# Attention and gated network in one kernel: a planner that looks ahead, one more group computed apart, a changed order of two loops, and projections that wait for fewer transfers

## The chip, the core and the metric

One core of a Trainium2 chip runs the whole program. The metric is the device time of one execution, the median of several. The engines are TensorE (PE: products of matrices, with its weight loads shown as PEld), VectorE (DVE), ScalarE (ACT), GpSimd (POOL) and SyncE (SP), which here issues the transfers.

## What is computed

First a linear attention: 8 batches, 8 heads, 576 tokens, head size 64, 128 features. Its result, 4608 tokens by 512, goes through a gated network with 1536 hidden columns. The arrays that come from `q`, `k`, `v` and `w_phi` are float32, the weights of the network float64.

```python
def phi(x):
    proj = np.einsum('bhsd,df->bhsf', x, w_phi)
    proj = proj - np.max(np.abs(proj), axis=-1, keepdims=True)
    return np.concatenate([np.exp(proj), np.exp(-proj)], axis=-1)
q_p, k_p = phi(q), phi(k)
kv, z = np.einsum('bhsf,bhsd->bhfd', k_p, v), np.sum(k_p, axis=2)
num = np.einsum('bhsf,bhfd->bhsd', q_p, kv)
den = np.einsum('bhsf,bhf->bhs', q_p, z)[..., None] + 1e-06
x = (num / den)             # then laid out as (4608, 512)
g = x @ w_gate
out = (g * (1.0 / (1.0 + np.exp(-g))) * (x @ w_val)) @ w_out
```

## The kernel before

**Heads.** Two heads make a pair, and 32 pairs are worked off in order by `attention(i, rank)`. For a pair, SP loads the keys, values and queries (L455 to L464, L582); of keys and queries the main part, 512 columns, comes in a first transfer and the last 64 in two small ones, one for each head. TensorE projects keys and queries (L354) in groups of columns, the last group being the tail. VectorE takes the largest magnitude (L502, L613) and subtracts it (L507, L618), ScalarE makes the exponentials, and TensorE the sums over keys (L546) and the numerators and denominators (L710). Then follows a chain: ScalarE copies the denominators out (L732), VectorE transposes them (L743) and takes the reciprocal (L744), GpSimd spreads it to all partitions (L748, L753), VectorE transposes it back (L757) and multiplies (L759). The result is x. Since the products take reduced operands, x is kept as a high part `xh` (ScalarE) and a low part `xl` (VectorE, L784), or, for later tokens, stored whole to `x_dram` (L774).

**Chunks.** The network works on 12 chunks c of 384 tokens and 12 groups f of 128 hidden columns. The first three chunks are made of the first 8 pairs, the "early" ones, and these run ahead of everything. For chunks 0 to 3 `first(c, f, low)` makes gate and value (a = 0 and 1, in the two banks `ps_gv`, gv in the trace) from four quarters k of the model's columns, where quarter k comes from the pair k of a batch. Each (a, k) is three products of 384 columns: high by high, high by low, low by high. Then ScalarE takes the tanh, and VectorE's L863 and L866 read the two banks, which frees them. `second` makes the output (L887 is the low part of the hidden values).

**Weights.** `weight_piece` turns a group's float64 weights into a high and a low part: ScalarE's L380, and on VectorE L381, L383, L386, L389, L391, L394 and, after ScalarE's copy, L397. Pieces of gate and value weights have 1024 columns (tile `a`), pieces of output weights 512 (`spare` or `m`). They are made once, while the early pairs run and after, and stored to `w_dram` for later loads.

**Pairs of chunks.** Chunks 4 to 11 go two by two through `block(c, f, ...)`, which makes the products of two chunks out of seven instead of eight and joins them with sums (L1112 is its product, L1122 and L1125 copy and join, L1045 loads its weights, L1061 loads x from `x_dram`). The generator `shared` calls the blocks: chunks 4 and 5, then 6 and 7, each over all f; then the last two pairs of chunks together. For f under LEAD only c_a (8 and 9) is computed; for f from LEAD to 11 c_a and c_b (10 and 11) follow one another and share the loaded weights (`held`); then c_b is computed for the f under LEAD, with those weights loaded again. A second phase behind it makes their outputs (L1359 and further).

**What sets the order.** No engine's order is written out by hand. The kernel adds steps to a `Plan`, each with an engine, a cost, the steps it comes after, and a rank. `Plan.run` goes through time by these costs: whenever an engine is free, it takes the ready step of lowest rank, whatever will become ready a moment later. What comes out is the fixed order of instructions on each engine. The waits between engines in the program follow from the data that the instructions read and write. An early pair's steps have its number as rank, 0 to 7; the steps of the network have -1 (FIRST), its loads -0.5 (NEXT), the products on TensorE 1000 and above, weight pieces 5, 6.5 and from 7.1 on. URGENT is -0.8. When TensorE has nothing ready in the plan, a filler product (L1484, L1487) is put there.

The rule in `first` for the order of the (a, k):

```python
order = [(a, k) for ks in ((0, 1, 2), (3,)) for a in range(2) for k in ks] if f == 0 else \
    [(a, k) for a in range(2) for k in range(NK)]
```

so for f = 0 the quarter k = 3 of both halves comes after the other three of both.

Of the kernel before, what the change touches and what calls it, by code (L numbers as in the profile page):

```python
# [23 lines left out]
NF = 128  # L24
# [28 lines left out]
LEAD = 4  # L53
# [3 lines left out]
URGENT = -0.8  # L57
OFFSETS = (0, -1, 0, 0, 0)


class Step:
    __slots__ = ("eng", "cost", "fn", "left", "then", "rank", "n", "lag", "take", "give", "key", "early")

    def __init__(self, eng, cost, fn, rank, n, lag, take, give, key):
        self.eng, self.cost, self.fn, self.rank, self.n, self.lag = eng, cost, fn, rank, n, lag
        self.take, self.give, self.key = take, give, key
        self.left, self.then, self.early = 0, [], 0


class Plan:  # L70
# [33 lines left out]
    def run(self):  # L104
        ready = {e: [] for e in self.LAG}
        busy = dict.fromkeys(self.LAG, False)
        for s in self.steps:
            if not s.left:
                heapq.heappush(ready[s.eng], (s.key, s))
        events, n, wire = [], 0, 0.0  # L110
        now = 0.0

# [3 lines left out]
        def start(e):  # L116
            nonlocal n, wire
            held = []
            got, saved = None, False
            while ready[e]:  # L120
                key, s = heapq.heappop(ready[e])
                if s.take is not None and (saved or len(s.take) > sum(len(x) for x in self.lists(s))):
                    held.append((key, s))
                    saved = True
                    continue
                got = s
                break
            for h in held:
                heapq.heappush(ready[e], h)
# [21 lines left out]
            for t in s.then:  # L151
                n += 1
                heapq.heappush(events, (freed if t.eng == e and e in ("ACT", "DVE", "PE", "POOL") else done, n, "dep", t))
# [11 lines left out]
        while events:  # L165
            now = events[0][0]
            while events and events[0][0] <= now:
# [3 lines left out]
                elif kind == "dep":  # L171
                    x.left -= 1
                    if not x.left:
                        heapq.heappush(ready[x.eng], (x.key, x))
                else:
                    b = self.bank[x]
                    (self.free if b < self.banks else self.extra if b < self.later else self.first).append(b)
# [46 lines left out]
def favor_attention_moe(ctx: ExitStack, tc: tile.TileContext, qT, kT, v, w_phi, wg, wv, wo, out):  # L224
# [209 lines left out]
    def keys_of(i, rank):  # L434
# [35 lines left out]
        for g, (t0, t1) in enumerate(GROUPS):  # L470
# [23 lines left out]
            after = [*k_in, last.get(("kv", i - (2 if early else 1)))]  # L494
# [68 lines left out]
    def attention(i, rank):  # L563
# [30 lines left out]
        if early:  # L594
            for g, (t0, t1) in enumerate(GROUPS):
# [16 lines left out]
                pj = add("PE", pe32(NF) if tail else w * pe32(256), project, q_in, rank, take=[key])  # L612
# [218 lines left out]
    def first(c, f, low):  # L831
# [5 lines left out]
        order = [(a, k) for ks in ((0, 1, 2), (3,)) for a in range(2) for k in ks] if f == 0 else \  # L837
# [701 lines left out]
```

## Time and profile before

| what | value |
|---|---|
| median of three runs | 1147.26 us (1146.52 to 1147.65) |
| profiled execution, its time | 1145.6 us |
| profiled execution, its span | 1143.8 us |
| ScalarE busy | 613.1 us, 54% |
| GpSimd busy | 156.4 us, 14% |
| bytes moved | 269.47 MB, mean 236 GB/s |

In the lines of the profile a line number L is that of the kernel's text; a product, an addition and so on stand with output <- inputs, buffer numbers left out, then the shape. A row of the timeline has its start in the span and its duration in us, both for the instruction or for the several merged into it; in brackets stands how long the engine was idle just before and who released it. A row of the waits has the sum in us, how often, and the longest. A row of windows has the stretch, its length, then the busy us of PE, PEld, DVE, ACT and POOL, the granted TensorE clock (1.00 is full), the share of time in which the DMA engines were busy, and GB/s.

### The profile page before, as it was taken

To read this page: it belongs to the slowest core of one execution; us is meant where nothing else is said; L and a number is where in the kernel's file an instruction comes from. 1 tells how busy PE (TensorE), PEld (TensorE's weight loads), DVE (VectorE), ACT (ScalarE), POOL (GpSimd) and SP (SyncE) were. 2 spreads that over 40 slices of the span, in tenths; PEclk is the share of its full clock that TensorE was granted. 3 is DMA by queue.
4 is the path that set the end of the run, shared out by engine and by line. 5 is a ranking of instruction groups with operands and counts; after the bars stand their busy time and mean duration, and the time that the engine had idled before them with its cause. 6 is when DMAs were issued, how large, how long until landed. Compare 5 with 4: busy or idle time off the path is not lost.

```text
span 1143.8 us, 25584 instructions
## 1 busy us (share of the span) xinstructions
PE 1129.0 (99%) x9842; PEld 1015.4 (89%) x9842; DVE 932.6 (82%) x1478; ACT 613.1 (54%) x1263; POOL 156.4 (14%) x385
## 2 busy tenths in 40 slices
PE   9999999999999999999999999999999999999998
PEld 7677999998777788888889988988999999999998
DVE  5999999998888788899889989986756566988663
ACT  6776333335766655676567655744434344544342
POOL 1111000002232323312311011010132000000000
PEclk9999999999999999999999999999999999999999
DMA  6546777856788776889988887877799878642511
GB/s 174 151 111 223 286 285 285 284 206 212 226 243 265 259 258 228 281 264 328 320 272 272 293 283 237 257 231 253 269 297 321 266 252 293 222 163 87 180 42 42
DMA packets 161705, 269.47 MB, mean 236 GB/s; under 512 B 56496, under 2 KB 106800, under 8 KB 158512
## 3 DMA queue, kind: packets, MB, share of 16 engines
q1 hardware_dynamic: 161120, 267.64, 71.0%
q8 instruction: 78, 1.28, 0.5%
q14 instruction: 43, 0.35, 0.1%
q10 hardware_dynamic: 464, 0.20, 0.1%
HBM read 187.56 MB, written 80.22 MB: 234 GB/s over the span
## 4 chain that ended last, share of the span: by engine, by line
PE 91%; DMA 4%; DVE 2%; SPq 1%; POOL 1%; issue 1%; ACT 1%; DVEq 0%; POOLq 0%; ACTq 0%
PE gv L354 17%; PE o L1112 14%; PE gv L1112 14%; PE o L354 10%; PE work L1359 7%; PE work L710 7%; PE work L354 6%; PE work L546 5%; PE gv L1359 5%; PE o L1359 4%; DMA w<-w_dram 2%; PE o L710 1%; PE o L546 1%; PE o L629 1%; DMA h_dram<-m 0%
## 5 line engine op out<-in xcount | busy, mean ns | idle before, releaser
L354 PE MATMUL gv<-xh,w 128*128 128x384 f32 x768 | 207.3, 338 | 3.0 <-DVE m L863 3.0
L354 PEld LDWEIGHTS gv<-xh,w 128*128 128x128 f32 x768 | 139.8, 188 | 7.4 <-DVE m L863 3.7
L354 PE MATMUL gv<-xl,w 128*128 128x384 f32 x384 | 128.7, 335 | 0.0
L354 PE MATMUL o<-w_hi,hidden 128*128 128x512 f32 x288 | 100.8, 400 | 0.0
L1112 PE MATMUL gv<-xh,w 128*128 128x384 f32 x336 | 98.8, 339 | 1.8 <-DVE w_hi L1231 1.1
L1112 PE MATMUL o<-m,w 128*128 128x384 f32 x388 | 80.8, 336 | 0.2 <-ACT snap L1122 0.2
L710 PE MATMUL work<-m,m 128*32 128x64 f32 (+2 forms) x1248 | 79.0, 400 | 0.0
L354 PEld LDWEIGHTS gv<-xl,w 128*128 128x128 f32 x384 | 72.1, 188 | 1.4 <-DVE xl L784 0.2
L1112 PEld LDWEIGHTS o<-m,w 128*128 128x128 f32 x388 | 68.4, 188 | 1.4 <-ACT snap L1122 0.6
L354 PEld LDWEIGHTS o<-w_hi,hidden 128*128 128x128 f32 x288 | 54.0, 188 | 14.3 <-issue 3.7
L710 PEld LDWEIGHTS work<-m,m 128*32 128x32 f32 x1248 | 30.2, 110 | 40.8 <-issue 34.4
L1112 PEld LDWEIGHTS gv<-xh,w 128*128 128x128 f32 x336 | 61.9, 188 | 4.8 <-issue 1.9
L1125 DVE TENSOR_TENSOR snap<-o,snap 128x384 f32<-128x384 f32 x72 | 39.9, 554 | 25.5 <-PE o L1112 20.4
L354 PE MATMUL o<-w_lo,hidden 128*128 128x512 f32 x144 | 56.8, 394 | 0.0
L1112 PE MATMUL o<-xh,w 128*128 128x384 f32 x188 | 54.9, 338 | 1.7 <-DMA w<-w_dram 1.7
L1112 PE MATMUL gv<-xl,w 128*128 128x384 f32 x168 | 56.4, 336 | 0.0
L1125 DVE TENSOR_TENSOR snap<-gv,snap 128x384 f32<-128x384 f32 x72 | 39.8, 552 | 20.2 <-PE gv L1112 14.0
L1122 ACT COPY snap<-o 128x384 f32<-128x384 f32 x72 | 34.3, 476 | 39.8 <-PE o L1112 25.8
L1122 ACT COPY snap<-gv 128x384 f32<-128x384 f32 x72 | 34.2, 475 | 36.7 <-PE gv L1112 21.2
L861 ACT ACTIVATE m<-gv 128x384 f32<-128x384 f32 x36 | 17.6, 490 | 66.3 <-PE gv L354 65.4
L531 ACT ACTIVATE m<-m 128x512 f32<-128x512 f32 (+1 forms) x88 | 45.7, 519 | 10.7 <-DVE m L507 10.6
L693 ACT ACTIVATE m<-m 128x576 f32<-128x576 f32 x48 | 31.4, 690 | 37.3 <-DVE m L686 37.3
(423 smaller groups left out, 3096.0 us busy)
## 6 DMA issues: line engine op xcount, KB each, us to landing
w<-w_dram SPq DMA_DIRECT2D x113, 512.0 KB, 5.6
h_dram<-m SPq DMA_DIRECT2D x90, 192.0 KB, 5.2
w_dram<-w SPq DMA_DIRECT2D x12, 1024.0 KB, 6.3
w_dram<-a SPq DMA_DIRECT2D x24, 512.0 KB, 4.4
w<-w_dram SPq DMA_DIRECT2D x12, 1024.0 KB, 6.8
w<-w_dram SPq DMA_DIRECT2D x38, 256.0 KB, 4.4
w_lo<-w_dram SPq DMA_DIRECT2D x36, 256.0 KB, 3.4
spare<-h_dram SPq DMA_DIRECT2D x19, 384.0 KB, 3.9
```

Of the source, the lines that this page charges most:

```text
L354: nc.tensor.matmul(o, l, r, start=a, stop=z)
L531: e0 = add("ACT", act(n * NF), lambda x=room: nc.scalar.activation(x[:, :, 0], x[:, :, 1], AF.Exp), after, rk)
L546: nc.tensor.matmul(ps_kv[r, n:n + (2 if tail else 1) * D2], x[:, r], y, start=g + m + k == 0, stop=tail and k == 1)
L629: nc.tensor.transpose(o[:, (h * w + t) * P:(h * w + t + 1) * P], y[:, 2 * t + h], ident)
L693: f0 = [add("ACT", act(S), f, [qc], rm) for h, f in enumerate(per_head(lambda h: nc.scalar.activation(qe[j][:, h], qx[j][:, h], AF.Exp)))]
L710: strips = lambda o, c, l, x, n, begin, final: nc.tensor.matmul(o[32 * n:32 * n + 32, c], l, x, start=begin, stop=final)
L861: s1 = add("ACT", act(CH), lambda: nc.scalar.activation(get(t_), ps_gv[0][:, :CH], AF.Tanh, scale=0.5), [ends[0], th_free[j]], FIRST)
L1112: nc.tensor.matmul(o[:, :CH], l, r, start=begin and i == 0, stop=i == len(terms) - 1, skip_group_check=True)
L1122: return add("ACT", act(CH), lambda: act_.copy(snap[n], bank[:, :CH]), [after, *snap_free[n]], FIRST)
L1125: return add("DVE", dve(CH), lambda: vec.tensor_tensor(out=snap[n], in0=bank[:, :CH], in1=snap[n], op=ALU.add), after, FIRST)
L1359: nc.tensor.matmul(cut(o, t - ts[0], W), l, r, start=begin and q == 0 and m == 0 and t == ts[0], stop=q == NQ - 1 and m == 2, skip_group_c ...
```

## The change

Four things change.

1. **The plan looks ahead** on ScalarE and VectorE. When all that a step of rank -0.8 or lower waits for has been started, the time at which it becomes ready is known (`at`), and it is put on a list `soon`. A step of another rank is begun only if it would end no later than OVER (150 ns) after the first of these times. If no step fits, the engine stays free for the urgent one, except when that is more than WAIT (150 ns) away: then the first of the steps that didn't fit is taken.
2. **LEAD is 5 instead of 4**, so f = 4 too is computed for c_a and c_b apart.
3. **The order of the (a, k) in `first`** that keeps k = 3 for last holds for f = 0 of chunk 1 only. Chunks 0, 2 and 3 now take all four quarters of a = 0, then those of a = 1.
4. **Projections that aren't tails wait in the plan only for the first transfer** of keys or queries, which holds all the columns that they read; tails still wait for all.

```diff
-LEAD = 4
+LEAD = 5
+OVER, WAIT = 150.0, 150.0
...
+        soon = {e: [] for e in ("ACT", "DVE")}
+
+        def fits(e, s):
+            if e not in soon or s.rank <= URGENT or not soon[e]:
+                return True
+            t = min(x.at for x in soon[e])
+            return now + s.cost <= t + OVER
...
+                if not fits(e, s):
+                    held.append((key, s))
+                    if late is None:
+                        late = s
+                    continue
                 got = s
                 break
+            if got is None and late is not None and min(x.at for x in soon[e]) > now + WAIT:
+                got = late
+                held = [h for h in held if h[1] is not late]
...
+                t.at, t.known = max(t.at, when), t.known + 1
+                if t.known == t.total and t.rank <= URGENT and t.eng in soon and when > now:
+                    soon[t.eng].append(t)
...
+                        if x.eng in soon and x in soon[x.eng]:
+                            soon[x.eng].remove(x)
...
-            after = [*k_in, last.get(("kv", i - (2 if early else 1)))]
+            after = [*(k_in if tail else k_in[:1]), last.get(("kv", i - (2 if early else 1)))]
...
-                pj = add("PE", pe32(NF) if tail else w * pe32(256), project, q_in, rank, take=[key])
+                pj = add("PE", pe32(NF) if tail else w * pe32(256), project, q_in if tail else q_in[:1], rank, take=[key])
...
-        order = [(a, k) for ks in ((0, 1, 2), (3,)) for a in range(2) for k in ks] if f == 0 else \
+        order = [(a, k) for ks in ((0, 1, 2), (3,)) for a in range(2) for k in ks] if f == 0 and c == 1 else \
             [(a, k) for a in range(2) for k in range(NK)]
```

What this does to the order of instructions is shown at three places. Line numbers of the changed kernel are 24 higher from the heads on.

**VectorE at the first early pair.** Before, from the last reduction of keys ahead of it (`m_0_84` holds the pair's denominators and numerators, `a_0_102` the first weight piece, `rc` is what GpSimd spreads):

```order
L502 TENSOR_REDUCE km_89<-o_104 128x4
L512 TENSOR_SCALAR km_89<-km_89 128x4
L381 TENSOR_SCALAR a_0_102<-a_0_102 128x1024
L743 STREAM_TRANSPOSE m_0_83<-m_0_84 128x288
L744 RECIPROCAL rp<-m_0_83 128x9
L383 TENSOR_SCALAR a_0_102<-a_0_102 128x1024
L618 TENSOR_TENSOR m_0_85<-gv_108,km_88 128x128
L386 SCALAR_TENSOR_TENSOR a_0_102<-a_0_101,a_0_102 128x1024
L757 STREAM_TRANSPOSE m_0_84<-rc 128x576
L759 TENSOR_TENSOR m_0_84<-m_0_84 128x576
L502 TENSOR_REDUCE km_90<-gv_107 128x4
```

and now:

```order
L526 TENSOR_REDUCE km_89<-work_111 128x4
L536 TENSOR_SCALAR km_89<-km_89 128x4
L767 STREAM_TRANSPOSE m_0_83<-m_0_84 128x288
L768 RECIPROCAL rp<-m_0_83 128x9
L781 STREAM_TRANSPOSE m_0_84<-rc 128x576
L783 TENSOR_TENSOR m_0_84<-m_0_84 128x576
L526 TENSOR_REDUCE km_90<-o_104 128x4
L531 TENSOR_TENSOR m_0_83<-o_104,km_90 128x4x128
L808 TENSOR_TENSOR xl_80<-m_0_84,xh_77 128x384
```

The first three steps of the weight piece (L381, L383, L386) stood around the pair's transposition and reciprocal. Now these come directly one after another with the back transposition behind them; the weight steps (L405 and so on) come at the second pair.

**VectorE at the last early pair** (`m_0_86` is that pair, `xl_81` and `xl_82` the low parts of chunks 1 and 2, `spare` a piece of 512 columns, `a_0_102` the third one of 1024). Before:

```order
L383 TENSOR_SCALAR spare<-spare 128x512
L743 STREAM_TRANSPOSE m_0_83<-m_0_86 128x288
L744 RECIPROCAL rp<-m_0_83 128x9
L386 SCALAR_TENSOR_TENSOR spare<-spare 128x512
L389 TENSOR_SCALAR spare<-spare 128x512
L391 SCALAR_TENSOR_TENSOR spare<-spare 128x512
L757 STREAM_TRANSPOSE m_0_86<-rc 128x576
L759 TENSOR_TENSOR m_0_86<-m_0_86 128x576
L394 TENSOR_TENSOR spare<-spare 128x512
L784 TENSOR_TENSOR xl_81<-m_0_86,xh_78 128x192
L381 TENSOR_SCALAR a_0_102<-a_0_102 128x1024
L784 TENSOR_TENSOR xl_82<-m_0_86,xh_79 128x384
```

and now:

```order
L405 TENSOR_SCALAR a_0_102<-a_0_102 128x1024
L407 TENSOR_SCALAR a_0_102<-a_0_102 128x1024
L421 TENSOR_TENSOR w_lo<-spare,w_hi 128x512
L767 STREAM_TRANSPOSE m_0_83<-m_0_86 128x288
L768 RECIPROCAL rp<-m_0_83 128x9
L410 SCALAR_TENSOR_TENSOR a_0_102<-a_0_101,a_0_102 128x1024
L413 TENSOR_SCALAR a_0_102<-a_0_102 128x1024
L781 STREAM_TRANSPOSE m_0_86<-rc 128x576
L783 TENSOR_TENSOR m_0_86<-m_0_86 128x576
L415 SCALAR_TENSOR_TENSOR a_0_102<-a_0_101,a_0_102 128x1024
L808 TENSOR_TENSOR xl_81<-m_0_86,xh_78 128x192
L808 TENSOR_TENSOR xl_82<-m_0_86,xh_79 128x384
```

Before, the piece in `a_0_102` began between the two writes of xl, and `w_lo` was written behind both. Now five steps of that piece (L405, L407, L410, L413, L415) and the write of `w_lo` stand ahead of the first.

**SP at the last loads of x from `x_dram`** (`w_72` to `w_74` and `a_2` are the buffers of weights). Before, from the two loads of x on:

```order
L1061 DMA spare<-x_dram 128x2x384 x2
L1045 DMA w_74<-w_dram 128x512
L1045 DMA a_2_8494<-w_dram 128x1024
L1045 DMA w_72<-w_dram 128x1024
L873 DMA h_dram<-m_1_1445 128x384
L1045 DMA a_2_8494<-w_dram 128x1024
L1045 DMA w_72<-w_dram 128x512
L873 DMA h_dram<-th 128x384
```

and now:

```order
L1085 DMA spare<-x_dram 128x2x384 x2
L1069 DMA w_73<-w_dram 128x1024
L897 DMA h_dram<-m_1_1450 128x384
L1069 DMA w_73<-w_dram 128x1024
L897 DMA h_dram<-m_1_1450 128x384
L1069 DMA w_74<-w_dram 128x1024
L1069 DMA w_74<-w_dram 128x512
L1069 DMA w_72<-w_dram 128x1024
L897 DMA h_dram<-m_1_1450 128x384
L1069 DMA w_72<-w_dram 128x1024
L897 DMA h_dram<-th 128x384
L1069 DMA w_73<-w_dram 128x1024
```

The two loads into `a_2` stood second and fifth behind the loads of x. Of those only one comes soon after, thirteen rows behind.

More of the change, by code (lines that the diff above doesn't have):

```diff
@@ L57 @@
 URGENT = -0.8
+OVER, WAIT = 150.0, 150.0
 OFFSETS = (0, -1, 0, 0, 0)
 class Step:
-    __slots__ = ("eng", "cost", "fn", "left", "then", "rank", "n", "lag", "take", "give", "key", "early")
+    __slots__ = ("at", "known", "total", "eng", "cost", "fn", "left", "then", "rank", "n", "lag", "take", "give", "key", "early")
     def __init__(self, eng, cost, fn, rank, n, lag, take, give, key):
@@ L66, in __init__ @@
         self.take, self.give, self.key = take, give, key
-        self.left, self.then, self.early = 0, [], 0
+        self.left, self.then, self.early, self.at, self.known = 0, [], 0, 0.0, 0
 class Plan:
@@ L107, in run @@
         for s in self.steps:
+            s.total, s.known, s.at = s.left, 0, 0.0
             if not s.left:
@@ L118, in start @@
             held = []
-            got, saved = None, False
+            got, saved, late = None, False, None
             while ready[e]:
@@ L152, in start @@
                 n += 1
-                heapq.heappush(events, (freed if t.eng == e and e in ("ACT", "DVE", "PE", "POOL") else done, n, "dep", t))
+                when = freed if t.eng == e and e in ("ACT", "DVE", "PE", "POOL") else done
+                heapq.heappush(events, (when, n, "dep", t))
+                t.at, t.known = max(t.at, when), t.known + 1
+                if t.known == t.total and t.rank <= URGENT and t.eng in soon and when > now:
+                    soon[t.eng].append(t)
             if s.give is not None:
```

## Prediction, made before the changed kernel was run

> **What bounds the kernel now.** I read the page's first part, then the windows, then TensorE's waits, and only where TensorE stands still did I go to the engine that it waits for.
>
> ```profile
> span 1143.8 us, 25584 instructions
> PE 1129.0 (99%) x9842; PEld 1015.4 (89%) x9842; DVE 932.6 (82%) x1478; ACT 613.1 (54%) x1263; POOL 156.4 (14%) x385
> PE 91%; DMA 4%; DVE 2%; SPq 1%; POOL 1%; issue 1%; ACT 1%; DVEq 0%; POOLq 0%; ACTq 0%
> ```
>
> The span less TensorE's busy time is 1143.8 - 1129.0 = 14.8 us. The change leaves TensorE's products as they are, so 14.8 us is all that it could win, and start-up and the last drain belong to it. What it can lose has no such bound. The windows say where the 14.8 us lie (PE, PEld, DVE, ACT, POOL busy us, then granted clock, DMA share, GB/s):
>
> ```profile
> 28.00:108.30 80.30, 78.14 (x1073) 57.22 (x1072) 74.98 (x147) 60.20 (x166) 12.29 (x42) 1.00 0.49 151
> 100.00:125.00 25.00, 21.99 (x209) 18.68 (x202) 23.64 (x42) 11.16 (x22) 1.94 (x6) 1.00 0.72 243
> 125.00:150.00 25.00, 25.00 (x143) 24.58 (x142) 23.58 (x37) 8.62 (x14) 0.00 (x0) 1.00 0.73 257
> 800.00:805.00 5.00, 2.55 (x14) 2.17 (x14) 2.50 (x4) 1.95 (x3) 0.00 (x0) 1.00 0.93 336
> 805.00:810.00 5.00, 5.00 (x29) 4.90 (x30) 2.82 (x5) 1.57 (x4) 0.00 (x0) 1.00 0.98 386
> ```
>
> Two places matter. From 28 to 108 us, while the eight early pairs of heads are made, VectorE is busy for 74.98 of 80.30 us, 93%: it is as full there as TensorE, and over the whole span (82%) one doesn't see it. Around 800 us TensorE loses half of a 5 us window while the DMA engines are at 0.93 to 0.98.
>
> TensorE at the end of the early stage:
>
> ```profile
> 108.75 0.44 PE L354 MATMUL gv<-xl,w 128*128 128x384 f32 x1
> 111.49 0.44 PE L354 MATMUL gv<-xh,w 128*128 128x384 f32 x1 [1.60 <-DVE m L863]
> 117.34 0.44 PE L354 MATMUL gv<-xh,w 128*128 128x384 f32 x1 [1.41 <-DVE m L863]
> ```
>
> The product at 108.75 is the first to read the low part xl of the last early pair (columns k = 3 of chunk 1). That pair's heads end here, and TensorE has nothing else queued that could run without it. VectorE writes that xl as the first row here:
>
> ```profile
> 108.34 0.35 DVE L784 TENSOR_TENSOR xl<-m,xh 128x192 fp32r<-128x192 f32 x1
> 108.61 0.69 DVE L381 TENSOR_SCALAR a<-a 128x1024 f32<-128x1024 f32 x1
> 109.21 0.56 DVE L784 TENSOR_TENSOR xl<-m,xh 128x384 fp32r<-128x384 f32 x1
> 109.68 0.69 DVE L397 TENSOR_TENSOR w_lo<-spare,w_hi 128x512 fp32r<-128x512 f32 x1
> 110.28 0.69 DVE L383 TENSOR_SCALAR a<-a 128x1024 uint32<-128x1024 uint32 x1
> 110.89 0.55 DVE L863 SCALAR_TENSOR_TENSOR m<-m,gv 128x384 f32<-128x384 f32 x1
> 112.01 1.22 DVE L386 SCALAR_TENSOR_TENSOR a<-a,a 128x1024 uint32<-128x1024 uint32 x1
> 113.27 0.69 DVE L389 TENSOR_SCALAR a<-a 128x1024 uint32<-128x1024 uint32 x1
> 113.99 1.23 DVE L391 SCALAR_TENSOR_TENSOR a<-a,a 128x1024 f32<-128x1024 uint32 x1
> 115.25 1.23 DVE L394 TENSOR_TENSOR a<-a 128x1024 f32<-128x1024 f32 x1
> ```
>
> It ends at 108.69 and the product that reads it starts at 108.75. So both engines arrive there together: whatever VectorE does more ahead of this step, TensorE waits for.
>
> **The change part by part.** Lines are those of the kernel before; in the changed one they stand 24 further down.
>
> *1. Steps of the weight pieces on VectorE.* The look-ahead moves them among the early pairs, and this is the term that decides. At pair 0 the weight step L381 stood ahead of the transposition L743, and VectorE with it:
>
> ```profile
> 18.59 3.12 PE L710 MATMUL o<-m,m 128*32 128x512 f32 x48
> 23.87 0.40 ACT L732 ACTIVATE m<-o 128x288 f32<-128x288 f32 x1
> 24.00 0.69 DVE L381 TENSOR_SCALAR a<-a 128x1024 f32<-128x1024 f32 x1 [2.69 <-ACT a L380]
> 24.61 0.47 DVE L743 STREAM_TRANSPOSE m<-m 128x288 f32<-128x288 f32 x1
> 27.98 0.78 DVE L757 STREAM_TRANSPOSE m<-rc 128x576 f32<-128x576 f32 x1 [0.76 <-POOL rc L753]
> ```
>
> The pair's numerators were done at 18.59 + 3.12 = 21.71. Without the weight step in the way, ScalarE's L732 can follow at once (0.40, to 22.1), and from L743 to L757 it takes 27.98 - 24.61 = 3.4 us, so L757 starts at about 25.5 instead of 27.98: **-2.5 us**. The three steps that were done inside this stretch (L381, L383, L386) now come later, between L757 and the last xl. Their prices, from start to the next start in the rows above: 0.60, 0.61, 1.26, together **+2.5 us**. These two cancel.
>
> What doesn't cancel is shown by the order of the rows near the last pair: ahead of its xl there stand in the changed kernel five more steps of a 1024-wide piece (L381, L383, L386, L389, L391) and one of a 512-wide one (L397), which before came after it. From start to next start: 0.60 + 0.61 + 1.26 + 0.72 + 1.26 + 0.60 = **+5.05 us**. The rows of both kernels agree in everything else ahead of that xl.
>
> In the stretch VectorE waited for one thing only:
>
> ```profile
> DVE m L757 <- POOL rc L753: 3.4, 5, 0.8
> ```
>
> Weight steps at other places could fill these five waits (-3.4 us), or uncover one at each of the seven pairs after the first (7 x 0.8 - 3.4 = +2.2 us). In the order, short work stands between L744 and L757 of these seven pairs in both kernels, some 1.9 to 3.7 us of it in the changed one by the durations above, so I take 0. Then the last xl ends at 108.69 + 5.05 = 113.7, and TensorE's work in front of it, the same as before, is done by about 108.3: **TensorE resumes 5.05 us later**. The bounds are +1.7 and +7.3.
>
> Nothing later pays this back by itself, for from 125 us on TensorE is busy all the time (25.00 of 25.00) with the same products. What it is paid with is weights that are ready earlier, and no row there shows TensorE waiting for them.
>
> *2. Two waits behind that place.* The first, 1.60 us before 111.49, is for L863, which frees the bank. Between the first xl and L863 VectorE had 110.89 - 108.61 = 2.28 us of steps; in the changed kernel the other L784 and L394 stand there, 0.47 + 1.15 = 1.62 us by the same rows (L394 is followed by L381 of the next piece, hence 116.40 - 115.25). **-0.6 us.** The second, 1.41 us, goes away: before, chunk 2 closed its first half's bank three products ahead of its end, with the new order twelve ahead. Twelve take 2.08 us (last row below), so the bank is read 9/12 x 2.08 = 1.6 us earlier, more than the 1.41. **-1.4 us.** For chunks 0 and 3 the same edit changes no wait that the trace shows: I cost it at nothing, for there is at least as much other work queued behind.
>
> ```profile
> 115.25 1.23 DVE L394 TENSOR_TENSOR a<-a 128x1024 f32<-128x1024 f32 x1
> 116.40 0.42 DVE L381 TENSOR_SCALAR m<-m 128x512 f32<-128x512 f32 x1
> 786.51 2.08 PE o L1112 x12
> ```
>
> *3. Projections that wait for one transfer.* They come a little earlier in TensorE's order at the start. Since VectorE sets the pace from pair 0 on, this is worth nothing beyond part 1. If VectorE didn't, it would be worth a part of what TensorE loses from 28 to 108 us, 80.30 - 78.14 = 2.2 us at most.
>
> *4. LEAD 5.* One more of the twelve column groups is computed for the two pairs of chunks apart, so its four groups of weights are loaded twice: three loads of 512 KB and one of 256 KB, 1.8 MB. The waits there:
>
> ```profile
> w<-w_dram SPq DMA_DIRECT2D x113, 512.0 KB, 5.6
> 796.63 8.12 DMA w<-w_dram
> 800.86 0.41 PE L1112 MATMUL gv<-xh,w 128*128 128x384 f32 x1 [0.75 <-DMA w<-w_dram]
> 804.89 0.41 PE L1112 MATMUL o<-xh,w 128*128 128x384 f32 x1 [1.71 <-DMA w<-w_dram]
> 883.88 0.41 PE L1112 MATMUL gv<-xh,w 128*128 128x384 f32 x1 [1.06 <-DVE w_hi L1231]
> ```
>
> A load that usually lands in 5.6 us took 8.12 when several were issued at once. In the order of the DMAs a large load that stood directly ahead of the late one, and another next behind it, now stand further on, which could remove the 0.75 and the 1.71; the wait before 883.88 stands behind a burst of loads as well (VectorE is only the last in the chain): 1.06, together -3.5 us at best. At worst the 1.8 MB come on top of engines that are full, at the 336 GB/s of the window that stalls: +5.4 us. Both pull with rows behind them; I take the middle, **+1.0 us**.
>
> *Sum.* 5.05 - 0.6 - 1.4 + 1.0 = **+4.1 us**. The profiled execution took 1145.6 us for its span of 1143.8, so a profile of the changed kernel should show about 1147.9. The median of the three runs is 1.7 us above the profiled one: 1147.26 + 4.1 = **1151.4 us**.
>
> **A rule weighed.** In all windows above the granted clock is 1.00, though TensorE stood still for 1.71 us at once; the new wait, from about 108.3 to 113.7, would be some 5 us in one piece, of which the trace of before has none. The Trainium skill, "TensorE: Matmul & The Clock Gate", under "What's actually happening", says that the clock falls to half after an idle window of about 3.4 us and comes back after as long a busy one. By that rule half of one such window is lost in addition, by my estimate 1.7 us. No run here shows it.
>
> **The rivals.**
>
> *A. VectorE closes up (not slower).* The extra steps cost nothing if VectorE runs from pair 0 to the last xl without a gap. It has 80.30 - 74.98 = 5.3 us of gaps there, about as much as the 5.05 us added. For it: look-ahead puts short steps where the waits for GpSimd were. Against: it takes the weight steps out of pair 0's wait, and 5.3 - 3.4 = 1.9 us of the gaps are not waits for GpSimd, but small gaps that order doesn't close. It decides at 5 us of gaps closed: then xl is as early as before, the 0.6 and 1.4 us remain, 1147.26 - 2.0 = 1145.3, and with waits for loads shrinking by up to 3.5 us, 1141.8. I name 1143.5.
>
> *B. The two ends meet (no change).* The early stage costs 5.05 - 2.0 = 3.1 us, and the waits around 800 to 884 us (3.5 us) all vanish because loads no longer bunch: 1146.9. For it: the large loads moved away from the late one. Against: more bytes in windows already at 0.93 and above.
>
> *C. Loads get worse.* The 1.8 MB come on top: 3.1 + 5.4 = +8.5, 1155.8.
>
> *D. The clock falls during the long wait.* TensorE then runs slower for a while after 113.7: with half of a stretch as long as the wait beyond 1.71 us (5.05 - 1.71 = 3.3 us) lost again, +1.7 on the forecast, 1153.1. This is the page's rule above, here as a mechanism of this place; all windows at 1.00 neither speak for nor against it.
>
> **How the numbers follow.** A difference under 0.2% (2.3 us) can't be told from no change here. The forecast (+1.7 to +7 us) has 0.52, A 0.15, B 0.15, C 0.10, D 0.08. Forecast, C and D are slower, but the low end of the forecast's own range is within 0.2%, which I count as 0.05. A lies mostly below 1145.0. Hence faster 0.13, same 0.22, slower 0.65. For the range I leave out the lower part of A and the end of C: 1145 to 1157. The forecast's own range is 1149 to 1155.
>
> **What would show it.** Part 1 is right if the last early pair's xl ends at 112 to 115 us, TensorE has a wait for DVE's xl of 3 to 6 us in front of the matching product, and the window from 100 to 125 us shows under 20 us busy. It is wrong if VectorE's wait for POOL vanishes and that xl comes by 109 us. Part 2 is right if only one wait for the gate's bank is left after it. Part 4 is judged between 740 and 900 us by the waits for w and by windows above 0.9. D is right if a window after the wait has a clock under 1.00. The prediction is wrong altogether if TensorE's order, not VectorE's, made the meeting at 108.7 us, that is, if TensorE now arrives there later too.

## The result, and the profile after

The changed kernel took **1159.03 us** (median of four runs, 1156.40 to 1160.47), the one before 1147.45 us beside it: a ratio of 1.0104, 95% interval 1.0085 to 1.0123. It is slower, as forecast, but by 11.6 us instead of 4.1, and outside the range. The profiled execution took 1159.84 us with a span of 1158.1, 14.3 us longer than that of before.

The first parts of the page (busy time of each engine, granted clock in 40 slices, chain that ended last):

```profile
span 1158.1 us, 25568 instructions
...
PE 1137.5 (98%) x9840; PEld 1021.0 (88%) x9840; DVE 937.2 (81%) x1478; ACT 614.8 (53%) x1263; POOL 155.0 (13%) x385
...
PEclk9998899999999999999999999999999999999999
...
PE 82%; DVE 8%; DMA 6%; POOL 2%; issue 1%; ACT 1%; SPq 1%; ACTq 0%; POOLq 0%; DVEq 0%
```

TensorE is busy for 8.5 us more with the same products: it ran some of them at a lower clock, and the clock's row says when, in the fourth and fifth slice, at 87 to 145 us. Another 5.8 us are new idle time. The windows of the early stage and two short ones within it (columns as before: busy us of PE, PEld, DVE, ACT, POOL, clock, DMA share, GB/s):

```profile
28.00:108.30 80.30, 76.29 (x966) 56.53 (x968) 74.39 (x146) 60.29 (x162) 12.04 (x36) 0.96 0.46 141
100.00:125.00 25.00, 18.16 (x161) 13.83 (x162) 20.86 (x34) 11.81 (x22) 2.26 (x6) 0.73 0.73 239
102.00:105.00 3.00, 2.17 (x7) 2.07 (x8) 2.96 (x8) 2.27 (x5) 0.00 (x0) 0.50 0.20 85
117.00:120.00 3.00, 2.46 (x7) 1.55 (x7) 2.88 (x6) 1.25 (x3) 0.00 (x0) 0.50 0.45 120
125.00:150.00 25.00, 25.00 (x140) 24.17 (x139) 23.76 (x37) 8.86 (x15) 0.00 (x0) 1.00 0.80 287
```

In the window from 100 to 125 us TensorE is busy 18.16 us (21.99 before), at a mean clock of 0.73. TensorE's timeline there, and at the one other place with a clock below 1.00:

```profile
102.83 0.69 PE L378 MATMUL gv<-xl,w 128*128 128x384 f32 x1 [3.36 <-DVE xl L808]
...
106.86 3.94 PE L734 MATMUL o<-m,m 128*32 128x512 f32 x48
...
116.73 0.69 PE L378 MATMUL gv<-xh,w 128*128 128x384 f32 x1 [3.47 <-ACT xh L806]
...
129.40 0.39 PE L378 MATMUL o<-w_hi,hidden 128*128 128x512 f32 x1
...
889.48 0.42 PE L1136 MATMUL o<-xh,a 128*128 128x384 f32 x1 [2.26 <-DMA a<-w_dram]
```

Two waits of 3.4 us for x stand where there were two of 1.5 us for a bank. Between them the last early pair's numerators (48 products in 3.94 us instead of 3.12) start at 106.86; before, they were done at about 102.7:

```profile
99.54 3.12 PE L710 MATMUL o<-m,m 128*32 128x512 f32 x48
```

And VectorE, which the prediction had as the bound:

```profile
25.87 0.78 DVE L781 STREAM_TRANSPOSE m<-rc 128x576 f32<-128x576 f32 x1 [1.42 <-POOL rc L777]
...
102.43 0.81 DVE L808 TENSOR_TENSOR xl<-m,xh 128x192 fp32r<-128x192 f32 x2
...
108.67 0.69 DVE L421 TENSOR_TENSOR w_lo<-spare,w_hi 128x512 fp32r<-128x512 f32 x1
...
111.32 0.48 DVE L767 STREAM_TRANSPOSE m<-m 128x288 f32<-128x288 f32 x1 [1.97 <-ACT m L756]
...
117.35 0.82 DVE L808 TENSOR_TENSOR xl<-m,xh 128x192 fp32r<-128x192 f32 x2
```

The first pair is 2.1 us earlier (L781 at 25.87), the last xl 9.0 us later (117.35 against 108.34). But VectorE isn't merely full there: ahead of the last early pair's transposition it waits 1.97 us for ScalarE, which waits for TensorE's late numerators.

**The lag.** To compare orders that differ I take one product that stands at the same place of the work in all of them, the first of the output weights (the row `o<-w_hi,hidden`). Before, it started here:

```profile
121.63 0.39 PE L354 MATMUL o<-w_hi,hidden 128*128 128x512 f32 x1
```

The changed kernel's starts at 129.40: a lag of **7.8 us** of the 14.3. From there to the end the changed kernel takes 6.5 us more: TensorE is busy for 1018.05 us instead of 1014.10, and idle for 2.5 us more. The new idle time is in its waits for centred keys between 280 and 600 us, of which before has none,

```profile
PE work L378 <- DVE m L531: 2.3, 4, 1.3
```

and in 1.2 us of longer waiting at 889 us (2.26 against 1.06), while other waits get about 1 us shorter. Behind the wait at 889 us the clock falls:

```profile
890.00:893.00 3.00, 3.00 (x12) 3.00 (x11) 0.00 (x0) 1.79 (x4) 0.00 (x0) 0.54 0.72 267
```

In the trace it is 0.50 from 890.22 to 893.64, which makes 1.7 us of the longer busy time. The other 2.2 us of that are not traced further.

### The profile page after: what moved, and what is told of

Same layout as the page of the kernel before. It is cut to its first block, busy times and chain, and to the rows that moved or that the text cites. A ratio compares the mean times of both kernels' runs of the same rounds, so it can differ in the third digit from the quotient of the medians.

```text
span 1158.1 us, 25568 instructions
## 1 busy us (share of the span) xinstructions
PE 1137.5 (98%) x9840; PEld 1021.0 (88%) x9840; DVE 937.2 (81%) x1478; ACT 614.8 (53%) x1263; POOL 155.0 (13%) x385
## 4 chain that ended last, share of the span: by engine, by line
PE 82%; DVE 8%; DMA 6%; POOL 2%; issue 1%; ACT 1%; SPq 1%; ACTq 0%; POOLq 0%; DVEq 0%
PE gv L378 17%; PE gv L1136 11%; PE o L1136 11%; PE o L378 10%; PE work L1383 7%; PE work L734 5%; PE work L378 5%; PE gv L1383 4%; PE o L1383 4%; PE work L570 4%; DMA w_dram<-a 2%; DMA w<-w_dram 2%; DVE km L526 1%; PE o L734 1%; DMA a<-w_dram 1%
## 5 line engine op out<-in xcount | busy, mean ns | idle before, releaser
L378 PE MATMUL gv<-xh,w 128*128 128x384 f32 x768 | 209.7, 342 | 3.7 <-ACT xh L806 3.5
L378 PEld LDWEIGHTS gv<-xh,w 128*128 128x128 f32 x768 | 141.8, 191 | 8.4 <-ACT xh L806 4.0
L378 PE MATMUL gv<-xl,w 128*128 128x384 f32 x384 | 130.4, 340 | 3.7 <-DVE xl L808 3.7
L1136 PE MATMUL o<-xh,w 128*128 128x384 f32 x316 | 92.7, 338 | 0.0
L1136 PE MATMUL gv<-m,w 128*128 128x384 f32 x364 | 77.0, 339 | 0.0
L1136 PEld LDWEIGHTS gv<-m,w 128*128 128x128 f32 x364 | 65.1, 190 | 0.5 <-issue 0.5
L1136 PE MATMUL gv<-xh,w 128*128 128x384 f32 x212 | 62.8, 340 | 2.1 <-DMA w<-w_dram 2.1
L1136 PEld LDWEIGHTS o<-xh,w 128*128 128x128 f32 x316 | 58.2, 188 | 0.7 <-issue 0.5
L1156 ACT ACTIVATE m<-snap 128x384 f32<-128x384 f32 x47 | 24.8, 527 | 55.1 <-DVE snap L1149 53.4
L1136 PE MATMUL o<-xl,w 128*128 128x384 f32 x158 | 53.1, 336 | 0.0
L1136 PE MATMUL o<-m,w 128*128 128x384 f32 x212 | 48.2, 337 | 0.4 <-ACT snap L1146 0.3
```

Source lines behind the costliest of these rows:

```text
L378: nc.tensor.matmul(o, l, r, start=a, stop=z)
L1136: nc.tensor.matmul(o[:, :CH], l, r, start=begin and i == 0, stop=i == len(terms) - 1, skip_group_check=True)
L1156: t0 = add("ACT", act(CH), lambda: act_.activation(get(t_), get(x), AF.Tanh, scale=0.5), [*after, th_free[j]], FIRST)
```

## The experiments

"Weight steps" is VectorE's work on weight pieces that stands ahead of the last early pair's xl, from the order of the rows and the durations in the prediction. Each ratio is against the kernel before in the same group of runs. A lag is read from the one profiled execution of its run, and it moves a little from execution to execution: only_lead has the early order of before row by row and yet 0.6 us, because the clock fell there behind a wait of 1.59 us, at a place where before waits 1.60 us and keeps 1.00:

```profile
111.27 0.45 PE L354 MATMUL gv<-xh,w 128*128 128x384 f32 x1 [1.59 <-DVE m L863]
113.00:115.00 2.00, 2.00 (x7) 2.00 (x7) 1.93 (x3) 0.00 (x0) 0.00 (x0) 0.50 0.73 282
```

| run | ratio (95%) | weight steps, us | lag, us |
|---|---|---|---|
| before | 1 | 19.9 | 0 |
| **changed kernel** | 1.0104 (1.0085 to 1.0123) | 24.8 | 7.8 |
| only_first | 1.0238 (1.0213 to 1.0263) | 27.1 | 11.1 |
| only_look | 1.0081 (1.0057 to 1.0105) | 19.9 | 0.0 |
| only_lead | 1.0025 (1.0012 to 1.0038) | 19.9 | 0.6 |
| only_order | 1.0026 (1.0012 to 1.0040) | 20.5 | 0.6 |
| no_first | 1.0005 (0.9985 to 1.0024) | 20.5 | 1.2 |
| no_look | 1.0126 (1.0097 to 1.0156) | 27.1 | 10.6 |
| pair1_only | 1.0097 (1.0061 to 1.0133) | 27.1 | 7.1 |
| pair0_only | 1.0144 (1.0121 to 1.0168) | 31.5 | 15.1 |
| warm5 | 1.0102 (1.0073 to 1.0130) | 24.8 | 7.1 |
| keep36 | 1.0066 (1.0040 to 1.0092) | 24.8 | 6.3 |
| late_piece | 1.0055 (1.0037 to 1.0072) | 20.5 | 5.5 |
| late_keep | 1.0039 (1.0023 to 1.0056) | 20.5 | 3.6 |
| c1_late | 1.0131 (1.0100 to 1.0162) | 27.1 | 9.3 |
| both_late | 1.0065 (1.0043 to 1.0087) | 20.5 | 8.6 |
| xl_first | 1.0129 (1.0105 to 1.0154) | 32.7 | 14.2 |
| xl_late | 1.0082 (1.0058 to 1.0106) | 20.5 | 9.4 |
| order_keep | 1.0026 (1.0012 to 1.0039) | 20.5 | 1.8 |
| x_pool | 1.0013 (0.9999 to 1.0027) | 19.9 | -0.1 |

### Each part alone

The kernel before with one of the four parts. The shorter lists:

```diff
+            after = [*(k_in if tail else k_in[:1]), last.get(...)]
+                pj = add("PE", ..., project, q_in if tail else q_in[:1], rank, take=[key])
```

> Only the projections' shorter list of waits in the plan; everything else as before. The order shows 11 filler products at the start instead of 16, chunk 1's products ahead of the eighth pair's numerators, and 27 us of weight steps on VectorE ahead of the last xl instead of 20. Theory 1 (this edit spoils the early stage: cold start, chunk 1's products block the last numerators, two waits of over 3 us after which the granted clock falls to 0.5): slower by 7 to 10 us, 1154 to 1158, lag of about +8 us at 125 us of the span. Theory 2 (the look-ahead moved the weight steps, as the prediction put it): within 1.5 us of before.

The look-ahead (the whole of part 1, with LEAD 4, the old order and the full lists):

> Only the look-ahead. The early stage's rows are those of before (16 fillers, chunk 1 behind the eighth numerators, 20 us of weight steps). Theory 1: no lag at 125 us; TensorE gets some 2 to 3 us of new waits between 290 and 590 us for VectorE's centred keys (the non-urgent steps that are held back), so 1148.5 to 1150.5. Theory 2: lag of 5 to 8 us already at 125 us, 1153 to 1156.

```diff
-LEAD = 4
+LEAD = 5
```

> Only LEAD 5. Theory 1 (the last loads come late once more, and the clock falls after that wait): a wait for a load of over 2 us near 880 us with the clock at 0.5 behind it, less waiting around 800 us, in sum +1 to +3 us, 1148.5 to 1150.5. Theory 2 (LEAD is worth nothing by itself, the wait at 886 us came from the other edits' order): within 1 us of before, no window under 1.00 near 880 us.

```diff
-order = [...] if f == 0 else \
+order = [...] if f == 0 and c == 1 else \
```

> Only the order of quarter k = 3. Chunk 1's products come ahead of the eighth pair's numerators here too, but with 16 fillers and 20.5 us of weight steps as before. Theory 1 (the place of chunk 1's products matters by itself, since TensorE stands in order behind them): a wait of over 2 us for xl ahead of the last numerators and the clock at 0.5 behind it, +1 to +4 us, 1148.5 to 1151.5. Theory 2 (only VectorE's lateness matters): -1 to -2 us, since one of the two waits for the bank goes, 1145 to 1146.5.

No part alone is faster. **only_first** is by far the slowest, 27 us: its lag is 11.1 us, so theory 2 falls, and the time is far above theory 1's 7 to 10 us too. It loses more than the lag again further on, the largest pieces being two waits for loads near 818 and 883 us (the view of the waits: engine, line, what it waited for; us in total, times, longest):

```profile
PE gv L354 <- ACT xh L782: 5.5, 1, 5.5
PE gv L1112 <- DMA a<-w_dram: 5.1, 1, 5.1
PE gv L1112 <- DMA w<-w_dram: 4.2, 3, 2.8
PE gv L354 <- DVE xl L784: 3.8, 2, 3.4
```

**only_look** has VectorE's rows of before up to 99 us, the same weight steps ahead of the last xl, and no lag: by itself the look-ahead doesn't move the weight steps. It isn't free either: its 1156.54 us lie above theory 1's range, and most of its 8 us comes from two waits for loads, of 5.30 and 2.71 us, and not from the 2 to 3 us for keys that I expected (0.2 us between 280 and 640 us). The longer one:

```profile
812.52 0.66 PE L1136 MATMUL o<-m,a 128*128 128x384 f32 x1 [5.30 <-DMA a<-w_dram]
```

The load was issued at 805.47 behind two loads of x that had waited for a store of x (0.66 us for the product: the clock had fallen here too). **only_lead** is 0.25% slower, 2.8 us; that is inside theory 1's 1 to 3 us, but the median of ten runs, 1151.07, is 0.6 us above the range named for the time. Its profiled execution shows the wait that theory 1 expects, 4.69 us before 887 us, with a clock of 0.50 behind it. At 1153.65 us that execution is the slowest of the ten, so the others may have lost less there. **only_order** moves chunk 1's products ahead of the last numerators without harm to these, but its two waits for the bank become one of 2.26 us with a lower clock behind it, and the 1.4 us that I had booked aren't won. Its time lies in theory 1's range, yet not by theory 1's wait for xl, which isn't there.

The four ratios add up to 3.7%; together they make 1.0%. The parts don't add, since each makes the plan write another order for all the rest.

### One part undone

The changed kernel with the full lists again, and without the look-ahead (`fits` always says yes):

> The changed kernel with the projections waiting for all transfers in the plan again (look-ahead, LEAD 5 and the order of k = 3 stay). 16 fillers and 20.5 us of weight steps ahead of the last xl again. Theory 1 (this edit makes the early lag): lag at 125 us under 1.5 us instead of 7.8, no clock under 0.9 around 100 to 125 us, 1149 to 1155. Theory 2 (the look-ahead or the order makes it): the lag stays at 6 us or more, 1157 to 1160.

> The changed kernel without the look-ahead (every ready step fits); the rest stays. 27 us of weight steps ahead of the last xl instead of 25. Theory 1 (the look-ahead only softens what the shorter list of waits does): lag of 10 to 12 us at 125 us as with that edit alone, 1165 to 1176. Theory 2 (the look-ahead moved the weight steps and makes the loss, as the prediction put it): 1148 to 1154.

**no_first settles which part it is**: with look-ahead, LEAD 5 and the new order in place, but the full lists, the kernel is as fast as before (0.9985 to 1.0024), slightly faster than my theory 1 allowed. Its early window is that of before, 78.14 us of 80.30 (windows, then TensorE's timeline):

```profile
28.00:108.30 80.30, 78.14 (x1073) 57.21 (x1072) 74.62 (x147) 60.38 (x165) 12.29 (x43) 1.00 0.49 148
```

```profile
113.09 0.69 PE L378 MATMUL gv<-xh,w 128*128 128x384 f32 x1 [2.26 <-DVE m L887]
```

Around this wait the clock is 0.50 for 3.4 us (112.60 to 116.02), which theory 1 had excluded.

**no_look** keeps the lag of the shorter lists alone (10.6), so the look-ahead softens that lag by 2.8 us; the time, 1161.06, stays below theory 1's range, mainly because this plan has no wait for a load above 1.3 us where only_first's has two, of 2.8 and 5.1, each with a lower clock behind it.

The orders of some more variants, which were built but not run, show where the lists act. With full lists for all early pairs, or for the first two alone, every row on every engine is that of no_first. So it is the lists of the first two pairs, and of these the keys': with the queries' full and the keys' short, every row is that of the changed kernel; the other way round, every row is that of no_first. Each of the two pairs by itself:

```diff
+            after = [*(k_in if tail or i == 0 else k_in[:1]), ...    # pair1_only
+            after = [*(k_in if tail or i != 0 else k_in[:1]), ...    # pair0_only
```

(and the same for the queries).

> The changed kernel with the shorter list for every pair but the first; from the third pair on it changes no row, so this is the second pair's alone. 16 fillers at the start as before, 27 us of weight steps ahead of the last xl. Theory 1 (the weight steps ahead of the last xl set the lag; 25 us of them gave 7.8 us, 27 gave 10.6 and 11): a lag of 9 to 11 us at 125 us, 1159 to 1164. Theory 2 (the start with 11 fillers and a cold clock is a large part): a lag under 7 us, 1154 to 1158.

> The changed kernel with the shorter list for the first pair alone: 11 fillers at the start, and 31.5 us of weight steps ahead of the last xl. Theory 1: a lag of 12 to 15 us at 125 us (33 us of weight steps gave 14.2), 1162 to 1168. Theory 2 (only the second pair's place matters, and the first pair's costs just the cold start): a lag of 1.5 to 4 us, 1150 to 1154.

Either suffices, and pair0_only is worse than both together. More weight steps come with more lag in this row of runs: 20.5, 24.8, 27.1, 31.5 us with 1.2, 7.8, 7.1 to 11.1, 15.1. They aren't all of it: further down, runs with the short lists and only 20.5 us still lag by 3.6 to 9.4 us. pair1_only's lag lies below theory 1's range: with 16 fillers and the same 27.1 us it has 7.1 us against 10.6 and 11.1 for those with 11.

### The start

In the changed kernel the plan thinks that the first keys are there earlier and puts 11 fillers ahead of them:

```profile
1.06 2.72 PE L1508 MATMUL gv<-nil 128*128 128x256 f32 x11 [1.06 <-DVE nil L347]
4.69 3.75 PE L378 MATMUL gv<-wbd,m 128*128 128x256 f32 x8 [0.91 <-DMA wbd<-in_w_phi_dram]
```

and before:

```profile
1.06 3.78 PE L1484 MATMUL gv<-nil 128*128 128x256 f32 x16 [1.06 <-DVE nil L323]
4.89 2.35 PE L354 MATMUL gv<-wbd,m 128*128 128x256 f32 x8
```

Eight products take 3.75 us, where they took 2.35 before behind 16 fillers, although the view gives the granted clock as 1.00 in both. It has nothing to go by there: the trace's record of the clock begins at 9.59 us in the changed kernel, and at 5.68 before. With five fillers more by hand:

```diff
+        for _ in range(5):
+            nothing()
         plan.run()
```

> The changed kernel with five more filler products at TensorE's start, 16 as before; nothing else moves. Theory 1 (with 11 fillers TensorE stands still for 0.9 us before the first data and then runs its first projections at half speed until 9.5 us, 427 ns for a product of 256 columns instead of 213): the first numerators at 18.6 us instead of 20.1, all of the early stage 1 to 1.5 us earlier, 1156 to 1158. Theory 2 (VectorE sets the pace from there on, so the start is covered): no change at 125 us, 1158 to 1160.

The projections run in 1.97 us and the first numerators start at 19.0 instead of 20.1, but only 0.6 us of that reaches the lag, and the time can't be told from the changed kernel's: theory 2, mostly.

### The weight steps, the clock, and the order of chunk 1

**late_piece** makes the first VectorE step of the pieces from f = 2 on wait for the early pairs; **keep36** puts products by zeros into the two waits; **late_keep** does both.

```diff
-            out=e(), in0=e(), ..., op1=ALU.min), [s0], rank)
+            out=e(), in0=e(), ..., op1=ALU.min), [s0, *(early_done if f > 1 else ())], rank)   # late_piece
...
+                if c == 1 and f == 0 and a == 0 and k in (2, 3):
+                    for _ in range(36):
+                        nc.tensor.matmul(ps_gv[a][:, CH:CH + P], nil, nil, start=True, stop=True, ...)   # keep36
```

In keep36 these products begin sums of their own in the bank, which disturbs chunk 1's gate sums of the first group; late_keep only adds zeros (`start=False`).

> The changed kernel with 36 products by zeros, some 2 us, ahead of each of the two long waits for xl (99 and 113 us), into columns of the bank that nobody reads; the order stays. Theory 1 (the clock falls to 0.5 because TensorE stands still too long, and half of some 5.7 us is lost behind each wait): the granted clock stays at 1.00, 3 to 5 us are won, 1154 to 1156. Theory 2 (VectorE is late by itself, and TensorE at half speed only fills time that it would wait anyway): the clock stays at 1.00, yet 0 to 1 us is won, 1158 to 1160.

> The changed kernel, with VectorE's steps of the weight pieces from the third group on made to wait for the early pairs: 20.5 us of weight steps ahead of the last xl instead of 24.8; 11 fillers, and chunk 1's products ahead of the last numerators, stay. Theory 1 (the weight steps ahead of the last xl are the price, as the prediction's first part had it): the lag at 125 us falls from 7.8 to 2 to 4 us, 1152 to 1156. Theory 2 (the place of chunk 1's products and the cold start make it): the lag stays at 6 to 8 us, 1157 to 1160.

> The changed kernel with the weight pieces from the third on after the early pairs, and with 36 products by zeros, some 2 us, added to unused columns of the bank ahead of each of the two places where TensorE waits for xl. Theory 1 (behind the weight steps the fallen clock is the next price): granted clock 1.00 from 90 to 125 us and a lag at 125 us of 3 to 4.5 us against 5.5 without these products, 1150 to 1153. Theory 2 (TensorE at half speed only fills time in which it would wait for VectorE anyway): clock 1.00, lag 5 to 6 us, 1153 to 1155.

late_piece takes 5 us off the time (1153.86) with 4.3 us fewer weight steps, half of what the change costs, but the lag only falls to 5.5, between the two theories. The rest comes later: its profiled execution, the fastest of nine at 1149.82 us, has neither the wait before 889 us nor a lower clock there. keep36 takes off as much (1153.62, just below both ranges), 1.4 us of it in the lag. Its clock isn't 1.00 all the way: it is 0.50 once more from 118.41 to 121.82, behind waits of 0.5 and 0.9 us. Further on its wait before 885 us is 0.9 us instead of the 2.26 before 889, with no lower clock behind it. In late_keep nothing is left under 1.00 in the window,

```profile
100.00:125.00 25.00, 24.37 (x249) 21.58 (x249) 21.06 (x36) 11.69 (x23) 1.06 (x6) 1.00 0.70 233
```

and the lag is 3.6: behind late_piece the fallen clock is worth 2.0 us. TensorE's largest wait left there is 0.63 us, since the zeros fill the others.

Two edits aimed at that rest. **c1_late** lets chunk 1's first products wait for the last numerators in the plan, as they stood before; **xl_first** lets the eighth pair's key steps on VectorE wait for the seventh pair's xl. **both_late** and **xl_late** are these with late_piece.

```diff
+                if c == 1 and f == 0:
+                    wait.append(last["nu", EARLY_PAIRS - 1])                                          # c1_late
...
-            [kproj, last.get(("km", 3 * i + g - 4))], freeing)
+            [kproj, last.get(("km", 3 * i + g - 4)), *(last["num", i - 1] if i == EARLY_PAIRS - 1 else ())], freeing)   # xl_first
```

> The changed kernel, with chunk 1's first products made to wait for the last early pair's numerators, as they stood before. The plan then puts 27 us of weight steps ahead of the last xl. Theory 1: the lag at 125 us is still 6 us or more, in one wait instead of two, 1156 to 1162. Theory 2 (TensorE, standing in order behind chunk 1, holds up the last numerators, and that is the price): the lag falls to 2 to 4 us, 1152 to 1155.

> The changed kernel with both of these: weight pieces from the third on after the early pairs (20.5 us ahead of the last xl), chunk 1's first products behind the last numerators; 11 fillers. Theory 1 and 2 alike: what is left is the cold start, a lag of 0.5 to 2.5 us at 125 us, 1149 to 1153. If more than 4 us of lag stay, the cause is earlier, in the pairs themselves.

> The changed kernel, with VectorE's key steps of the eighth pair made to wait for the seventh pair's xl. Chunk 1's products come still earlier, and the plan puts 33 us of weight steps ahead of the last xl. Theory 1 (the weight steps ahead of the last xl are the price): a lag at 125 us of 10 to 15 us, 1161 to 1168. Theory 2 (the seventh pair's xl, behind the eighth pair's keys on VectorE, is the price): the wait near 99 us goes and the lag is under 6 us, 1152 to 1157.

> Both: the eighth pair's key steps behind the seventh pair's xl, and the weight pieces from the third on after the early pairs (20.5 us of weight steps ahead of the last xl). If the two causes add up (theory 1 and 2 together), the lag at 125 us is 1 to 3 us, 1148 to 1151. If it stays at 5 us or more, the rest lies in the eighth pair's own chain, whose keys and queries come after both.

None of the four lowers the lag below that of its counterpart. In c1_late TensorE stands no longer at xl, but for 6.0 us at the eighth pair's centred queries:

```profile
PE o L653 <- DVE m L642: 6.0, 1, 6.0
```

and both_late has the same wait with 20.5 us of weight steps. both_late and xl_late keep lags of 8.6 and 9.4 us, above the 4 and 5 us that I had named as the sign that the rest lies in the pairs themselves. So beyond weight steps and clock the eighth pair's last queries are late on VectorE, whichever product TensorE meets first. The row is the subtraction in their last 128 columns, here in before, no_first, the changed kernel and late_piece:

```profile
93.97 0.29 DVE L618 TENSOR_TENSOR m<-work,km 128x128 f32<-128x128 f32 x1
96.01 0.28 DVE L642 TENSOR_TENSOR m<-work,km 128x128 f32<-128x128 f32 x1
103.48 0.29 DVE L642 TENSOR_TENSOR m<-o,km 128x128 f32<-128x128 f32 x1
103.31 0.29 DVE L642 TENSOR_TENSOR m<-o,km 128x128 f32<-128x128 f32 x1
```

In the first two it stands ahead of the ninth pair's keys and the seventh pair's xl, in the last two behind both. The eighth pair's numerators need it; they start at 99.54, 100.08, 106.86 and 105.94. How much of the 3.6 us of late_keep this makes, no run separates: they stay open.

### Two that failed

**order_keep**, on the kernel before with the new order of k = 3, adds 20 products by zeros against the lower clock there. **x_pool**, also on the kernel before, has GpSimd issue the loads of x (`nc.gpsimd.dma_start`), so that SP doesn't stand in front of loads of weights.

> The kernel before with the new order of k = 3 alone, and 20 products by zeros, some 1.2 us, added to unused columns of the bank ahead of chunk 1's k = 3 and of chunk 2's first product, where that edit alone leaves one wait of 2.26 us and a clock of 0.93 in the window from 100 to 125 us. Theory 1 (the edit saves a wait of 1.4 us and the fallen clock eats it): clock 1.00, lag at 125 us 0 or below, 1.0 to 1.5 us faster than the edit alone, 1145.5 to 1148. Theory 2 (the wait is VectorE's and stays): no difference to the edit alone, 1148 to 1150.

> The kernel before, with the loads of x from x_dram issued by GpSimd instead of SP; no other row moves. Theory 1 (the loads of weights land late near 800 us because SP stands in front of the loads of x until the store of x has landed, 2.6 us): SP doesn't wait there, the 0.75 and 1.71 us of TensorE's waits near 800 us go, 1144.5 to 1146.5 against 1147.5 to 1148. Theory 2 (the DMA engines are full there): the waits stay within 1 us, no change.

order_keep holds the clock at 1.00 from 100 to 125 us, but its zeros had to wait 1.0 us for L866, which reads that bank, and the lag grew to 1.8. x_pool removes SP's wait, and of TensorE's 0.75 and 1.71 us near 800 us one wait of 1.2 us is left, under another name: for ScalarE's split of x (L1071), which landed later itself. From 770 to 900 us TensorE's waits are 3.1 us in sum instead of 3.5, and the time doesn't change, as theory 2 has it.

## Why the prediction was wrong

**The step that failed is part 3**, the projections that wait for one transfer: "worth nothing beyond part 1". Undone by itself (no_first) it takes the whole loss away, from a ratio of 1.0104 to 1.0005, and by itself (only_first) it costs 2.4%. I priced it as a shift of a few products, and ascribed the moved weight steps to the look-ahead. only_look has none of them ahead of the last xl (19.9 us, as before), and the shorter lists bring them, with and without it. The order of the rows had been read for the change as a whole, and that can't say which part moved a row.

**Part 1** had a right mechanism, a third weight piece ahead of the last xl, and the right place. Pair 0 came 2.1 us earlier (2.5 forecast). It took all other rows ahead of that xl to agree in both kernels; in their order they don't, since the eighth pair's last queries went behind the ninth pair's keys. And the weight steps show less than the 5.05 us: late_piece takes 4.3 us of them away and the lag falls by 2.2. The forecast had one wait, with TensorE resuming 5.05 us later; there were two, and the last xl ended at 117.70, 9.0 us later than before and outside the 112 to 115 us named for it. What I passed over was TensorE's order: chunk 1's products now stand ahead of the last numerators, so the first wait delays these, and TensorE itself comes to the place of the second wait at 113.3 us instead of 108.3. That was the sign named for a prediction that is wrong altogether. c1_late shows that moving the products back is no cure, as the eighth pair's last queries were late by then in any case.

**Rival D, the clock,** was given 0.08 and 1.7 us. It came true twice in the early stage and once at 890 us. In the two early stretches TensorE is busy for 5.74 and 4.95 us at 0.50, half of which, 5.3 us, is lost on it; 1.4 us (keep36, which leaves one short stretch) to 2.0 us (late_keep against late_piece) are seen in the lag. The Trainium skill's rule ("TensorE: Matmul & The Clock Gate", "What's actually happening") speaks of an idle window of about 3.4 us. Behind waits of about that length, 3.36 and 3.47 us, the clock was low, but it had fallen 2.3 and 2.1 us after they began. 2.26 us sufficed three times (before 889.48 us, in no_first and in only_order) and 1.59 us once, in only_lead. On the other side 1.60 and 1.71 us in before left the clock at 1.00, and so did 2.56 us in pair0_only, before 841.62. So below some 2.6 us the length of a wait alone doesn't decide it here.

**Part 2:** two waits for the bank became waits for x, and one of 0.21 us was left; the gains were there but lay inside longer waits. With the full lists (no_first, only_order) they merge into one of 2.26 us, so of the 2.0 us booked at most 0.75 was won in waiting, and the clock behind it gave back more: a lag of 0.6 to 1.2 us is left, little more than one execution's fall of the clock makes in only_lead.

**Part 4**, +1.0 us, was too low: alone it costs 0.25%, 2.8 us. The wait before 887 us in only_lead, 4.69 us, lies within my bound of 5.4, and the clock behind it I hadn't counted. In no_first, which has LEAD 5 too, there is no such wait.

**The median:** the profiled one stood 1.9 us under the median before and 0.8 us above it after, so the profiles differ by 14.3 us and the medians by 11.6.

## What to carry to other kernels

Where a planner fixes the order, an edit to what the plan believes is an edit to every row behind it: build each part alone and compare orders before costing any of them at nothing. On a TensorE that is 99% busy, look at the length of single waits and not only at their sum: behind the start, every wait of more than 2.6 us in these traces and some of 1.6 to 2.6 us were paid again in clock. A shorter wait in the plan is no gain where the real transfer is hardly waited for (0.2 us for keys in the first 130 us of before); here it only changed the order of everything behind it.

## What the runs showed of the hardware

- One idle stretch of 2.26 us let the clock fall. In no_first the products behind it start 0.32 us apart instead of 0.17 (0.69 us for the first instead of 0.44), from the moment TensorE resumes; at 889.48 the fall came only some 0.7 us after it. Waits of the same kind don't always do it: 1.59 us did in only_lead, 2.56 us in pair0_only didn't.
- Between the start and the end of TensorE's work, the stretches at 0.50 in these traces last 3.41, 6.83 or 10.24 us, one, two or three times the same length: 890.22 to 893.64 and 101.75 to 108.57 in the changed kernel, 115.41 to 125.65 in no_look.
- At the start products ran at half speed (0.43 us from one of 256 columns to the next instead of 0.22) until 9.5 us with 11 fillers and one pause of 0.91 us, and until 5.6 us with 16, while the view gave a clock of 1.00: the record of the clock begins only there. With 16 fillers it begins at 3.92 us in warm5 and at 6.79 in no_first, so this point moves from run to run.
- Loads that GpSimd issued instead of SP landed in 7.8 and 8.6 us, where SP's two had taken 4.0 and 4.6. The DMA engines' share was 0.97 and 1.00 in the windows 795 to 800 and 800 to 805 us, 0.87 and 0.93 before; whether the issuer or this load made the difference, no run separates.
